# Block 0's first loads, the V blocks, the reciprocals and the last divisions of an adaLN transformer block put at other places in the program order

## The chip, the core and the metric

The kernel runs on one core of a Trainium2 chip. A core has five engines, each with its own instruction queue, worked off in order: TensorE (PE in the profile; its weight loads, PEld, overlap its matmuls), VectorE (DVE), ScalarE (ACT), GpSimd (POOL) and SyncE (SP), which here only issues DMAs. The metric is the device time of one execution in microseconds; lower is better. A measurement is a median of several runs.

## The reference, cut to what matters

`S = 2048` rows of width `D = 512`; attention with `H = 32` heads of 16; a feed-forward part of width 1792.

```python
mod = (_silu(c) @ w_mod).reshape(c.shape[0], 6, 1, -1)
sa, ca, ga, sb, cb, gb = (mod[:, i] for i in range(6))
h = _layernorm(x) * (1 + ca) + sa
qkv = (h @ wqkv)...                                # q, k, v of 32 heads of 16
p = _softmax(einsum("bhqd,bhkd->bhqk", q, k) * 16 ** -0.5)
x = x + ga * (einsum("bhqk,bhkd->bhqd", p, v)... @ wo)
h = _layernorm(x) * (1 + cb) + sb
x = x + gb * (gelu_tanh(h @ w1 + b1) @ w2 + b2)
```

## The kernel before

**Units and steps.** Queries are cut into 4 blocks of 512 rows (`NB`), heads into 8 groups of four. A pair of both is a *unit*: 32 units (`NU`), block by block. A unit goes over the 2048 keys in 16 *steps* of 128 keys (`NKC`), so the main loop has 512 steps (`half_step(hs)`, hs 0 to 511). A step has

- 4 score matmuls `e` (keys x queries) of its keys, each followed by an exponential on ScalarE (`p`); every exponential advances a counter, the *tick* (`advance`), so that a step has 4 ticks;
- 4 matmuls `mx` (queries x keys) of a later unit, 20 steps ahead, each followed by a reduction on VectorE to row maxima. When a unit has all 64 of them, `max_rows` combines them, POOL splits them in two parts, and they go to DRAM and back into two extra rows of the queries' tile `qst`, so that the score matmul itself subtracts them. The store is put 3 ticks, the load 6 ticks behind. For unit u this falls at the end of step 16u-5;
- the value matmuls `pv` of the step before, at the end of the step (`pv_step`), into one PSUM bank for the whole unit. At steps hs that are multiples of 16 this is the last step of a unit, and `attn_out` copies the bank to SBUF (`osb`) and sends it out;
- up to 6 *background* matmuls `bg` on half of the rows (`bg_mm`, `RUN`), from a generator of groups: in `block0` the projections of q, k and v, then per block of rows the output projection (`front`), the norm and the feed-forward part (`feed`). A group of 24 such matmuls takes four steps. A group starts only in an even step. A generator that yields `None` leaves the step without background.

**The order** is written by hand. `later(n, f)` runs `f` n ticks on; `sides` holds transposes of which one goes into a step. DMAs are all issued from SP's queue in program order. While the background fills the steps, each weight tile is fetched by `wload` into a ring of eight.

**Where the change bites.**

- `block0` ends when its last projection is stored (step 140 in the trace). `open_ffn` then takes over the memory of the staging tiles; four `wload` calls fetch the output weights `wo`; the generator waits `OPEN` ticks; `front(0)` has the rows x fetched into `x2` 9 ticks after that.
- V blocks: VectorE transposes the projected V in four blocks (`turn_blocks`, `turn_block`), two in each of two steps, from the single tile `vr`.
- `o_prep(b, k)` prepares the output projection of block b, a quarter k at a time: it loads denominators and sums, takes a reciprocal on VectorE (`inv`), sends it to DRAM (`store`), gets it back spread over the rows (`load`) and divides (`div`: a product, a cast and a difference on POOL; in the tail, `over`, on VectorE).
- `front(0)` after its four groups: the statistics and norm of the rows (`stat`, `factor`, `norm`) and four transposes (`trans`), each of 4 matmuls into a bank of the `mx` ring, a ScalarE pass and two POOL operations. The feed-forward groups follow when three are issued.
- A gelu is made in two halves (`ffn1`): a ScalarE pass and three POOL operations; 9 ticks later a tanh on ScalarE and four POOL operations (`second`).
- When the maxima of all units are done (step 492 on), the steps have no `mx` matmuls, four background matmuls and two exponentials in advance. From step 507 on no background group starts, and what is left of the feed-forward part of block 2 and all of block 3 run in a tail after the loop.

Of the kernel before, what the change touches and what calls it, by code (L numbers as in the profile page):

```python
# [10 lines left out]
AF = mybir.ActivationFunctionType  # L11
# [12 lines left out]
KC = D // P  # L24
NB = 4
# [34 lines left out]
Y202.a X1 x*2  # L60
"""
RUN = 6
OPEN = 12
WB = 8
FIRST = {"h32": 4, "pf": 1, "vr": 3}
STAGE = {"pf": 1, "vr": 1, "wraw": 2, "wf": 1}
# [6 lines left out]
def block_kernel(ctx: ExitStack, tc: tile.TileContext, x, wqkv, wo, w1, b1, w2, b2, c, w_mod, out):  # L73
# [276 lines left out]
    def turn_blocks(hs):  # L350
        if not blocked:
            return
        if until_hs[0] is None:
            until_hs[0] = hs + 1
        left = until_hs[0] - hs
        n = len(blocked)
        rowed_now = rowed[0] >= clock["t"] - 4
        for _ in range(n if left <= 0 else 0 if rowed_now and n <= 2 * left else -(-n // (left + 1))):
            turn_block()
# [66 lines left out]
        return reduce  # L426

    rows, rowed = {}, [0]

    def max_rows(u):  # L430
        rowed[0] = clock["t"]
# [272 lines left out]
    def attn_out(u, pv):  # L704
        qb, g = divmod(u, NG)
        o = kqpool.tile([P, TB], F32, tag="osb", name="osb", bufs=1)
        saw(ve.tensor_copy(o, pv))
        rowed[0] = clock["t"]
        late = u < NU - 1
        later(2 * late, lambda: sy.dma_start(ou_d[qb][g], o))  # L710
        if g % 2:
            later((4 if 0 < qb < NB - 1 and g == NG - 1 else 8) * late, lambda: ready.append((qb, g // 2)))
# [36 lines left out]
            return pools["f"].tile([P, D], F32, tag="t", name=name, bufs=8)  # L749
        return dvpool.tile([P, D], F32, tag="t", name=name, bufs=4)  # L750

    free_pc, busy, over = [0], [0], [False]

    def o_prep(b, k):

        dn = small.tile([P, 32], F32, tag="dn", name="dn")
        base = ou_d[b]
        sy.dma_start(dn, base[2 * k : 2 * k + 2].rearrange("g (j r) (a f) -> (g j) r a f", r=32, f=32)[:, DH])
        ob, rb = tmp("ob"), tmp("rb")
        for g in range(2):  # L760
            sy.dma_start(ob[g * 64 : (g + 1) * 64], base[2 * k + g].rearrange("(j r) t -> j r t", r=32)[:, :DH])
        eng = ve if over[0] else gp
        r = rden_d[b][k * 8 : (k + 1) * 8]
        busy[0] += 1

        def inv():
            ve.reciprocal(dn, dn)
            later(0 if over[0] else 2, store)

        def store():  # L770
            sy.dma_start(r.rearrange("h (a f) -> (h a) f", f=32), dn)
            later(1 if over[0] else 5, load)
            if over[0]:
                wload()

        def load():
            sy.dma_start(rb, bass.AP(tensor=r.tensor, offset=r.offset, ap=[[TB, 8], [0, DH], [1, TB]]))
            later(9 if over[0] else 3 if fast else 7, div)
            if k == KC - 1:
                later(2, lambda: close_by.__setitem__(b, True))  # L780
            if over[0]:
                for _ in range(6):
                    wload()
                load_x2(last, x2)

        def div():
            eng.tensor_tensor(ob, ob, rb, op=ALU.mult)
            eng.tensor_copy(pc(b, k, 0), ob)
            eng.tensor_tensor(pc(b, k, 1), ob, pc(b, k, 0).bitcast(F32), op=ALU.subtract)
            done[b] += 1  # L790
            busy[0] -= 1

        fast = 0 < b < NB - 1 and k == KC - 1
        later(11 if over[0] else 28 if b == 0 and k < KC - 1 else 9 if fast else 14, inv)

    def try_prep():
        if not ready or not pcs:
# [15 lines left out]
    for b in range(NB):  # L813
# [3 lines left out]
            at = top  # L817
        if b < NB - 1:
            stream += [(b + 1, "o", k) for k in range(KC)]
    wt, used, ringed, extra = {}, set(), [], []  # L820

    def wload():

        n = len(wt)
        if n == len(stream) or "f" not in pools:
            return
        key = stream[n]
        if extra:
            t = extra.pop()
        elif len(ringed) < WB or ringed[-WB] in used:  # L830
            t = pools["f"].tile([P, 2, D], FR, tag="w", name=f"w{key[1]}", bufs=WB)
            ringed.append(key)
        else:
            return
        sy.dma_start(t.bitcast(F32), {"o": wo_d, 1: w1_d, 2: w2_d}[key[1]][key[2]])
        wt[key] = t
# [19 lines left out]
    def front(b, x2):  # L856


        later(9, lambda: load_x2(b, x2))
        yield from until(lambda: close_by[b])  # L860
        yield from loaded(b, *[("o", k) for k in range(KC)])
        mv = small.tile([P, 4, 2], F32, tag="mv", name="mv")
        rs = {}
        xn = {}

        def norm(t):
            xn[t] = tmp("xn")
            (gp if b or t < 3 else ve).tensor_scalar(
                xn[t], x2[t], mv[:, t, 0:1], rs[t], op0=ALU.subtract, op1=ALU.mult)
            later(40 if b else 72, lambda: gp.tensor_tensor(x2[t], x2[t], b2_b, op=ALU.add))  # L870
            if len(xn) == 4:
                later(5, lambda: sides.extend([lambda fc=fc: trans(fc, "mx") for fc in range(KC)]))

        def stat(t):
            if b == 0 and t == 3:
                ln_stat(mv, t, x2[t])
                later(1, lambda: factor(t))
                return
            st = small.tile([P, 2, 6], F32, tag="bsh", name="bsh")

            def part(i):
                ve.bn_stats(st[:, i], x2[t][:, i * HD : (i + 1) * HD])

            def whole():
                ve.bn_aggr(mv[:, t], st)
                factor(t)

            def calm(f):
                later(3, f) if rowed[0] > clock["t"] - 4 else f()

            n = 4 if t < 3 else 3
            calm(lambda: [part(0), later(n, lambda: calm(lambda: [part(1), later(n, lambda: calm(whole))]))])

        def factor(t):
            rs[t] = small.tile([P, 1], F32, tag=f"rt{t}", name=f"rt{t}")
            ve.tensor_scalar(rs[t], mv[:, t, 1:2], EPS, None, op0=ALU.add)
            gp.tensor_tensor(rs[t], rs[t], mhalf[:, 0:1], op=ALU.pow)
            later(3 if t < 3 else 2, lambda: norm(t))

        for t in range(4):  # L900

            def evac(ps, t=t):
                y = tmp("y")
                ac.activation(y, ps, AF.Copy)

                def add():
                    gp.tensor_tensor(x2[t], y, x2[t], op=ALU.add)
                    later(8 if t < 3 else 4 if b else 3, lambda: stat(t))

                later(2, add)  # L910

            yield o_terms(b, t, range(KC)), "bg", evac
        drop(b, *[("o", k) for k in range(KC)])

        def trans(fc, bk):
            ps = take(bk)
            for t in range(4):
                te.transpose(ps[:, t * P : (t + 1) * P], xn[t][:, fc * P : (fc + 1) * P], ident)  # L918
            h = tmp("h32")
            ac.activation(h, ps, AF.Identity, scale=modc[:, 1, fc, 0:1], bias=modc[:, 1, fc, 1:2])  # L920
            gp.tensor_copy(pc(b, fc, 0), h)
            gp.tensor_tensor(pc(b, fc, 1), h, pc(b, fc, 0).bitcast(F32), op=ALU.subtract)
            turned[fc] = clock["t"]

        turned = {}
        yield "ln"
        yield from until(lambda: len(turned) >= KC - 1)

    def feed(b, x2):
# [7 lines left out]
        def ffn1(i):  # L937
            def evac(ps):
# [14 lines left out]
                def second():  # L953
# [5 lines left out]
                    gp.tensor_tensor(g[:, 1], h, g[:, 0].bitcast(F32), op=ALU.subtract)  # L959
                    gt[i] = g, clock["t"]  # L960

                later(9, second)

            wi = wt[b, 1, i].rearrange("p a (k n) -> p a k n", n=P)
# [40 lines left out]
    def block0():  # L1005

        plan = [(1, 1, [3]), (2, 1, [0, 1, 2, 3])]
        plan += [(w, k, range(1 if w == 0 else NB)) for k in (2, 3) for w in (0, 1, 2)]
        plan += [(0, k, range(1, NB)) for k in range(KC)]

        def fetch(n):
            if n < len(plan):
                w, k, _ = plan[n]
                load_w(w, k)
                soon(12, lambda: split_w(w, k, wslots[n % 4]))

        for key in [k for k in wt_of if k not in ((1, 1), (2, 1))]:
            wt_of.pop(key)
        for n, (w, k, bs) in enumerate(plan):
            if not pcs and not any(0 in p[2] for p in plan[n:]):  # L1020
                open_pc()
            yield from until(lambda: (w, k) in wt_of)
            fetch(n + 2)
            for b in bs:
                yield proj_v(k, b) if w == 2 else proj_qk(w, k, b, n == len(plan) - 1 and b == NB - 1)
            wt_of.pop((w, k))
        yield from until(lambda: not preps and not owed[0] and not blocked and not vrows and not busy[0])
        open_ffn()
        for k in range(KC):
            wload()  # L1030
        yield from wait(OPEN)

    pools["old"] = [dvcm, scm, wcm, hcm]

# [28 lines left out]
    def saw(ins):  # L1063

        if act["g"] and not act["g"]["seen"]:
            act["g"]["seen"] = ins.ins
# [285 lines left out]
```

## Time and profile before

| | us |
|---|---|
| timed runs | 1698.67, 1684.69, 1686.91; median 1686.91 |
| the profiled execution | 1683.93 |
| its span, first to last instruction | 1682.1, mean granted TensorE clock 0.993 |
| main loop, first to last value matmul | 106.3 to 1563.6 |
| tail, from the last value matmul | 1563.6 to 1682.1 |

In rows of the groups of instructions, "busy, mean ns of one" stands behind the count, then the idle time of the engine before them and what ended it. In rows of the time line the first number is the start in us from the span's start, the second the duration; brackets give the engine's idle time before it and its releaser. In rows of the chain a DMA's time runs from its issue to its landing. In rows of windows stand, after the stretch and its length, the busy times of PE, PEld, DVE, ACT and POOL with the count of instructions, the granted TensorE clock as a share, the DMA engines' busy share and the GB/s that they moved. In what follows, step n is the stretch that ends where the value matmuls of `half_step(n)` start; it holds the score matmuls of that step.

### The profile page before, as it was taken

What the parts mean: (1) busy time and instruction counts of PE and PEld (TensorE: products, weight loads), DVE (VectorE), ACT (ScalarE), POOL (GpSimd) and SP (SyncE); (2) the same over time, 40 slices, a digit from 0 to 9 for tenths busy, and PEclk for the clock granted to TensorE, in tenths of its full rate; (3) what the DMA queues carried; (4) which work ended last, traced back from release to release, by engine and by line L of the source; (5) the groups of instructions that cost most, each with busy time, mean ns of one, the idle gap of its engine ahead of it and who ended that gap; (6) DMA issues with size and microseconds to landing.
All of it is one profiled execution on the core that took longest, in us unless ns stands there. A gap on an engine that the chain in (4) does not pass through costs nothing.

```text
span 1682.1 us, 32274 instructions
## 1 busy us (share of the span) xinstructions
PE 1656.0 (98%) x12079; PEld 905.8 (54%) x12079; DVE 1424.9 (85%) x2770; ACT 1211.3 (72%) x2320; POOL 716.7 (43%) x719
## 2 busy tenths in 40 slices
PE   7999999999998999999999999999999999999999
PEld 6655555555544455555555555555555555553677
DVE  7999999999898999999999899999999899990332
ACT  4367777777776788778777888778777887788131
POOL 7443544534221376216523476126434475056210
PEclk8999999999999999999999999999999999999999
DMA  8766666665546443335462554254452643252544
GB/s 289 212 196 181 222 214 207 224 175 191 152 146 200 119 113 102 78 97 142 115 170 59 152 156 106 68 141 138 106 152 56 185 128 84 64 166 72 185 152 159
DMA packets 142808, 246.97 MB, mean 147 GB/s; under 512 B 25390, under 2 KB 53052, under 8 KB 142652
## 3 DMA queue, kind: packets, MB, share of 16 engines
q1 hardware_dynamic: 140896, 243.80, 49.8%
q8 instruction: 96, 1.57, 0.4%
q10 hardware_dynamic: 1756, 1.11, 0.3%
q14 instruction: 60, 0.49, 0.1%
HBM read 184.56 MB, written 60.29 MB: 146 GB/s over the span
## 4 chain that ended last, share of the span: by engine, by line
PE 93%; DMA 3%; DVE 2%; POOL 1%; ACT 0%; SPq 0%; issue 0%; POOLq 0%; ACTq 0%; DVEq 0%
PE bg L279 40%; PE pv L720 29%; PE e L685 16%; PE mx L415 4%; PE pr L279 2%; DMA wraw<-in_A_wqkv_dram 1%; DVE mxp L420 1%; PE o L279 1%; DMA qk<-parts 0%; DVE hTlo L510 0%; PE mx L918 0%; DMA m<-m 0%; DMA wt<-wos 0%; POOL wqkv L210 0%; DMA qst<-m 0%
## 5 line engine op out<-in xcount | busy, mean ns | idle before, releaser
L420 DVE TENSOR_REDUCE mxp<-mx 128x1 f32<-128x512 f32 x2038 | 1288.1, 682 | 116.7 <-PE mx L415 102.2
L692 ACT ACTIVATE p<-e 128x512 f32<-128x512 f32 x2048 | 1072.4, 608 | 307.9 <-PE mx L415 265.6
L415 PE MATMUL mx<-kh,qst 48*128 48x512 f32 x2038 | 842.2, 424 | 0.7 <-DVE mxp L420 0.5
L685 PE MATMUL e<-qst,kh 50*128 50x512 f32 x2048 | 777.3, 423 | 10.6 <-DMA qst<-m 5.3
L685 PEld LDWEIGHTS e<-qst,kh 50*128 50x128 f32 x2048 | 342.4, 185 | 440.6 <-ACT p L692 327.2
L720 PE MATMUL pv<-p,vg 128*17 128x512 f32 x4096 | 541.1, 599 | 0.1
L415 PEld LDWEIGHTS mx<-kh,qst 48*128 48x128 f32 x2038 | 369.8, 185 | 18.8 <-DVE mxp L420 9.4
L279 PE MATMUL bg<-w,g 64*128 64x512 f32 (+1 forms) x1080 | 269.7, 389 | 0.0
L279 PEld LDWEIGHTS bg<-w,g 64*128 64x128 f32 (+1 forms) x1080 | 200.4, 186 | 30.8 <-POOL g L958 0.9
L279 PE MATMUL bg<-pchi,w 64*128 64x512 f32 x672 | 182.9, 391 | 0.0
L720 PEld LDWEIGHTS pv<-p,vg 128*17 128x17 f32 x4096 | 68.2, 95 | 170.6 <-issue 168.8
L279 PE MATMUL bg<-hThi,wqkv 64*128 64x512 f32 x560 | 153.4, 393 | 0.0
L279 PEld LDWEIGHTS bg<-pchi,w 64*128 64x128 f32 x672 | 123.9, 185 | 23.0 <-DVE tick L1135 5.1
L279 PEld LDWEIGHTS bg<-hThi,wqkv 64*128 64x128 f32 x560 | 103.9, 186 | 12.4
L956 POOL TENSOR_SCALAR s<-s 128x512 f32<-128x512 f32 x42 | 62.9, 1497 | 82.5 <-ACT s L954 81.7
L279 PE MATMUL bg<-pclo,w 64*128 64x512 f32 x336 | 91.9, 392 | 0.0
L975 POOL TENSOR_TENSOR x<-y,x 128x512 f32<-128x512 f32 x28 | 36.0, 1286 | 125.5 <-ACT y L974 125.5
L279 PE MATMUL bg<-hTlo,wqkv 64*128 64x512 f32 x280 | 76.2, 391 | 0.0
L949 POOL TENSOR_TENSOR s<-h 128x512 f32<-128x512 f32 x42 | 43.8, 1042 | 74.9 <-ACT h L948 74.9
L279 PEld LDWEIGHTS bg<-pclo,w 64*128 64x128 f32 x336 | 61.7, 185 | 14.5 <-DVE tick L1135 3.4
L279 PE MATMUL bg<-wo,pchi 64*128 64x512 f32 x192 | 60.4, 395 | 0.0
L437 POOL CAST m<-mt 128x32 fp32r<-128x32 f32 x32 | 6.8, 212 | 123.1 <-DVE mt L435 123.1
(162 smaller groups left out, 1359.3 us busy)
## 6 DMA issues: line engine op xcount, KB each, us to landing
kh<-qk SPq DMA_DIRECT2D x256, 192.0 KB
w<-w2s SPq DMA_DIRECT2D x56, 512.0 KB
w<-w1s SPq DMA_DIRECT2D x54, 512.0 KB
qk<-parts SPq DMA_DIRECT2D x32, 512.0 KB
vg<-v SPq DMA_DIRECT2D x48, 272.0 KB
qst<-qk SPq DMA_DIRECT2D x64, 192.0 KB
qk<-parts SPq DMA_DIRECT2D x32, 256.0 KB
ou<-osb SPq DMA_DIRECT2D x32, 256.0 KB
```

The lines of the kernel that those rows point to most:

```text
L279: return te.matmul(ps, term[0][r], rhs, start=i == 0, stop=i == n - 1)
L415: te.matmul(ps, qst[u][r0 : r0 + KR, p, qc * P : (qc + 1) * P], kh(u, kr // 2)[r0 : r0 + KR, p, (kr % 2) * TB : (kr % 2 + 1) * TB], start= ...
L420: ins = ve.tensor_reduce(mxp[u][:, hc, kr : kr + 1], ps, axis=AX.X, op=ALU.max, negate=True)
L437: gp.tensor_copy(m2[:, 0], mt)
L685: ins = te.matmul(ps, kh(u, kc // 8)[r0 : r0 + KX, p, (kc % 8) * P : (kc % 8 + 1) * P], qst[u][r0 : r0 + KX, p], start=True, stop=True)
L692: op = ac.activation(t, ps, AF.Exp, scale=SCALE)
L720: te.matmul(pvb[32 * j : 32 * j + VW], vg[u % 2][:, n : n + VW], pt.pop(4 * s + j), start=kc == 0, stop=kc == NKC - 1)
L949: gp.tensor_tensor(s, h, h, op=ALU.mult)
L956: gp.tensor_scalar(s, s, 1.0, None, op0=ALU.add)
L975: later(4, lambda: gp.tensor_tensor(x2[t], y, x2[t], op=ALU.add))
```

## The change

- `block0` now waits `WAIT` = 6 ticks after `open_ffn` before it has the weights fetched (`wready` keeps the step's own `wload` calls back until then), fetches x of block 0 in the same place, and waits the other 8 of `OPEN` = 14 ticks.
- In the step at a unit's end `turn_blocks` turns no block.
- `calm`, which was local to the statistics, is shared: it puts an operation off by 2 ticks (it was 3) while VectorE has just been given a unit's combined maxima or copy, and now also in a unit's last step before `pv_step`. The reciprocals go through it.
- `attn_out` copies on ScalarE where no background group is under way.
- In `front(0)` the transposes are no longer all `sides`: two are given to the generator as steps of their own, in the background's bank, and the other two go as `sides` into the same two steps.
- The divisions of the last block wait (`behind`) for a tick that is 1 to 3 behind a gelu's first half, or more than 20 behind.

```diff
-OPEN = 12
+OPEN = 14
+WAIT = 6
...
         if until_hs[0] is None:
             until_hs[0] = hs + 1
+        if hs % NKC == 0:
+            until_hs[0] += 1
+            return
...
+    def calm(f):
+        if rowed[0] > clock["t"] - 4 or cur["pv"] % NKC == NKC - 1:
+            later(2, lambda: calm(f))
+        else:
+            f()
...
     def attn_out(u, pv):
         qb, g = divmod(u, NG)
         o = kqpool.tile([P, TB], F32, tag="osb", name="osb", bufs=1)
-        saw(ve.tensor_copy(o, pv))
-        rowed[0] = clock["t"]
+        if act["g"]:
+            saw(ve.tensor_copy(o, pv))
+            rowed[0] = clock["t"]
+        else:
+            ac.activation(o, pv, AF.Copy)
...
         def load():
             sy.dma_start(rb, bass.AP(tensor=r.tensor, offset=r.offset, ap=[[TB, 8], [0, DH], [1, TB]]))
-            later(9 if over[0] else 3 if fast else 7, div)
+            later(9 if over[0] else 3 if fast else 7, behind if b == NB - 1 and not over[0] else div)
...
+        def behind():
+            n = clock["t"] - gelu[0]
+            if over[0] or 1 <= n <= 3 or n > 20:
+                div()
+            else:
+                later(1, behind)
...
-        later(11 if over[0] else 28 if b == 0 and k < KC - 1 else 9 if fast else 14, inv)
+        later(11 if over[0] else 28 if b == 0 and k < KC - 1 else 9 if fast else 14, inv if over[0] else lambda: calm(inv))
...
     def wload():
         n = len(wt)
-        if n == len(stream) or "f" not in pools:
+        if n == len(stream) or "f" not in pools or not wready:
             return
...
     def front(b, x2):
-        later(9, lambda: load_x2(b, x2))
+        if b:
+            later(9, lambda: load_x2(b, x2))
...
             if len(xn) == 4:
-                later(5, lambda: sides.extend([lambda fc=fc: trans(fc, "mx") for fc in range(KC)]))
+                later(5, lambda: sides.extend([lambda fc=fc: trans(fc, "mx") for fc in range(KC)]) if b else normed.append(True))
...
-            def calm(f):
-                later(3, f) if rowed[0] > clock["t"] - 4 else f()
...
         yield "ln"
+        if b == 0:
+            yield from until(lambda: normed)
+            for fc in range(0, KC, 2):
+                sides.append(lambda fc=fc: trans(fc + 1, "mx"))
+                yield lambda fc=fc: trans(fc, "bg")
+            yield from until(lambda: len(turned) >= KC - 1)
+            return
         yield from until(lambda: len(turned) >= KC - 1)
...
+                gelu[0] = clock["t"]
                 later(9, second)
...
         open_ffn()
+        yield from wait(WAIT)
+        wready.append(True)
         for k in range(KC):
             wload()
-        yield from wait(OPEN)
+        load_x2(0, pools["x2"][0])
+        yield from wait(OPEN - WAIT)
```

More of the change, by code (lines that the diff above doesn't have):

```diff
@@ L750, in tmp @@
         return dvpool.tile([P, D], F32, tag="t", name=name, bufs=4)
-    free_pc, busy, over = [0], [0], [False]
+    free_pc, busy, over, gelu = [0], [0], [False], [-99]
     def o_prep(b, k):
@@ L819, in block_kernel @@
             stream += [(b + 1, "o", k) for k in range(KC)]
-    wt, used, ringed, extra = {}, set(), [], []
+    wt, used, ringed, extra, wready = {}, set(), [], [], []
     def wload():
         n = len(wt)
-        if n == len(stream) or "f" not in pools:
+        if n == len(stream) or "f" not in pools or not wready:
             return
@@ L863, in front @@
         rs = {}
-        xn = {}
+        xn, normed = {}, []
         def norm(t):
```

## The prediction

> **What bounds the kernel now.** I read the page's busy shares and chain first, then the times at which the value matmuls `pv` start, which mark the 512 steps, then every step that is longer than its neighbours.
>
> ```profile
> PE 1656.0 (98%) x12079; PEld 905.8 (54%) x12079; DVE 1424.9 (85%) x2770; ACT 1211.3 (72%) x2320; POOL 716.7 (43%) x719
> ...
> PE 93%; DMA 3%; DVE 2%; POOL 1%; ACT 0%; SPq 0%; issue 0%; POOLq 0%; ACTq 0%; DVEq 0%
> ```
>
> TensorE is the bound, and the change takes no matmul away. So only the steps in which TensorE waits can give time back. The next rows (length, then busy time of each engine, granted clock, DMA share and GB/s; one row for one step, except the fifth) hold those steps and what they should be compared with.
>
> ```profile
> 539.92:542.75 2.83, 2.83 (x26) 1.49 (x30) 2.76 (x7) 2.56 (x6) 1.30 (x2) 1.00 0.01 2
> 502.31:504.91 2.60, 2.38 (x18) 0.81 (x17) 2.55 (x5) 2.07 (x6) 0.55 (x3) 1.00 0.60 228
> 510.11:519.42 9.31, 4.47 (x24) 2.51 (x22) 3.51 (x6) 3.08 (x6) 0.00 (x0) 0.69 0.86 288
> 519.42:522.87 3.45, 3.45 (x24) 1.62 (x23) 2.52 (x5) 1.69 (x4) 0.00 (x0) 0.84 1.03 243
> 508.30:514.10 5.80, 2.64 (x20) 0.81 (x16) 3.13 (x6) 2.26 (x5) 0.00 (x0) 0.97 0.99 385
> 148.74:152.08 3.34, 3.31 (x25) 1.60 (x23) 3.34 (x9) 2.57 (x6) 0.00 (x0) 1.00 0.08 28
> 239.90:243.24 3.34, 3.31 (x25) 1.62 (x23) 3.34 (x9) 2.59 (x6) 2.29 (x3) 1.00 0.70 225
> 331.12:334.46 3.34, 3.31 (x25) 1.60 (x23) 3.34 (x9) 2.57 (x6) 0.59 (x1) 1.00 0.33 100
> 194.50:197.46 2.96, 2.96 (x25) 1.62 (x23) 2.96 (x7) 2.20 (x5) 2.54 (x3) 1.00 0.29 81
> 840.12:843.26 3.14, 3.14 (x24) 1.62 (x22) 3.14 (x8) 2.38 (x6) 0.00 (x0) 1.00 0.17 57
> 1206.56:1209.72 3.16, 3.16 (x24) 1.62 (x22) 3.16 (x8) 2.41 (x6) 0.00 (x0) 1.00 0.19 60
> 565.16:568.06 2.90, 2.60 (x18) 0.94 (x16) 2.87 (x8) 2.37 (x6) 2.80 (x2) 1.00 0.01 3
> 568.06:572.22 4.16, 3.65 (x21) 1.60 (x21) 4.16 (x9) 2.83 (x6) 0.56 (x1) 1.00 0.62 175
> 572.22:575.40 3.18, 2.96 (x22) 1.27 (x21) 2.72 (x5) 2.44 (x5) 1.89 (x2) 1.00 0.86 219
> 1513.35:1519.47 6.12, 3.07 (x20) 1.35 (x18) 1.71 (x6) 2.35 (x6) 5.53 (x8) 1.00 0.01 2
> 1519.47:1522.32 2.85, 2.85 (x17) 1.17 (x16) 0.16 (x1) 2.85 (x8) 2.62 (x4) 0.71 0.10 22
> 1522.32:1525.26 2.94, 2.94 (x16) 0.82 (x14) 0.16 (x1) 1.62 (x5) 1.17 (x1) 0.70 0.58 203
> 1529.48:1531.61 2.13, 2.13 (x18) 0.82 (x17) 0.85 (x2) 2.13 (x6) 1.66 (x2) 1.00 0.08 31
> ```
>
> An ordinary step with background matmuls takes 2.83 us, one without them 2.60. Two places stand out: step 144, the first of unit 9 (9.31 us), and step 492, the first after all maxima are done (6.12 us).
>
> **Step 144: output weights and x.** The queue of that place, and the landings that the chain shows:
>
> ```profile
> 502.90 0.46 SPq L302 DMA_DIRECT2D qk<-parts  x1
> ...
> 506.37 1.75 SPq L835 DMA_DIRECT2D wo<-wos  x4
> ...
> 508.17 1.16 SPq L442 DMA_DIRECT2D m<-m  x2
> ...
> 510.11 1.05 PE L720 MATMUL pv<-p,vg 128*17 128x512 f32 x8
> ...
> 514.32 0.57 SPq L448 DMA_DIRECT2D qst<-m  x2
> ...
> 515.99 0.76 PE L685 MATMUL e<-qst,kh 50*128 50x512 f32 x1 [4.83 <-DMA qst<-m]
> ```
>
> ```profile
> 416.13 1.95 DMA m<-m
> 418.13 2.81 DMA qst<-m
> ...
> 502.90 3.40 DMA qk<-parts
> ...
> 508.76 5.50 DMA m<-m
> 514.32 1.54 DMA qst<-m
> ```
>
> The four weight loads (512 KB each) go out at 506.37, as soon as the last projection has landed (502.90 + 3.40), and they stand in front of the store of unit 9's row maxima. That store takes 5.50 us instead of the 1.95 of unit 7; the maxima then reach the queries too late, and TensorE waits 4.83 us. The wait also costs clock: the granted share is 0.69 in this step and 0.84 in the next.
>
> In the new order the block's end (step 140) waits 6 ticks; a tick is one exponential, four to a step. Loads of weights and x then come in step 142, behind the maxima's store (step 140) and load (step 141). Background restarts 6+8 ticks after the end, at step 144 at the earliest. Before, 12 ticks gave step 143, which is odd, and a group begins only in an even step: so OPEN 14 costs no step. Steps 144 and 145 should take 2.83 + 2.96 (the row at 194.50 is the step after a unit's end) instead of 9.31 + 3.45: 6.97 us gained.
>
> What is late next: the weights. The maxima's store is free of the weights but not of the projection, so it lands at 506.3 to 507; the loads of the maxima go out then, take 1.54 to 2.81 us and land at 508 to 510, ahead of 511.1, when unit 9's first score matmul is due (510.11 plus 1.05 for the value matmuls of step 143). The weight loads follow on the queue, from about 507.2. At 385 GB/s (fifth row) 512 KB take 1.36 us. With 1.5 us around them (3.40 us less 2.0 us for the projection's 768 KB), the first quarter lands at about 510.1 and the second at 511.4; they are wanted at about 511.5 and 512.2. No wait is the lower end; if the loads go out 2 us later, the wait is 2 us. I take 0.4: **gain 6.6, between 3.5 and 7.0** (3.5: a wait of 2 us, and 1.5 of clock, below). The Trainium skill gives a price for a transfer (DMA: Bandwidth & Descriptors, Anatomy of one DMA): about 2.0 us plus bytes over 436 GB/s. As an estimate from it the two quarters land at 510.4 and 511.6, so there would be no wait, and the sum below would be 0.4 us lower.
>
> x (4 loads, 1 MB) and the weights (2 MB) now also stand in front of K of unit 10. At 385 GB/s 3.1 MB take 8.2 us, so K lands near 518; its maxima want it in step 148, at 511.1 + 4 x 2.83 = 522.4. Hidden, with 4 us to spare.
>
> **V blocks and reciprocals.** The three steps of 3.34 us hold two block transposes ahead of the copy of the finished unit, the two of 3.14 and 3.16 a reciprocal; VectorE is busy all through each. A unit's end without either takes 2.96. The copy itself, and a small item for the next part:
>
> ```profile
> L707 DVE COPY osb<-pv 128x512 f32<-128x512 f32 x32 | 21.7, 677 | 15.2 <-PE pv L720 15.2
> ...
> L885 DVE BATCH_NORM_AGGREGATE mv<-bsh 128x2 f32<-128x12 f32 x11 | 2.2, 200 | 0.0
> ```
>
> Moved one step on, they meet a VectorE that has 2.83 - 2.76 = 0.07 us free, but three banks of maxima between it and TensorE. Gain 3 x 0.38 = **1.1** and 0.18 + 0.20 = **0.4**. If they only lengthen the next step, nothing is gained; a second lengthening would cost as much (bounds -1.5 to 1.5). I take the gain, because the copy frees the only `pv` bank and a transpose frees none. The V store goes out one step later; its rows are wanted several steps on. A reciprocal is two steps later, with its store, load and division; the projection needs the division four steps after that.
>
> **Block 0's gap, steps 160 to 165.** It has no background. The copy of unit 9 goes from VectorE (0.68) to ScalarE, where 2.37 of 2.90 us are used. But the last statistics of row block 2 now fall in step 160, a unit's end, and are put off by four ticks. They then complete the norm one tick after step 163 has begun, so the four transposes, two to a step, come in steps 164 and 165 and background restarts at step 166, as before. By rows: steps 161 and 162 were 2.90 + 4.16, VectorE busy throughout; without the copy (0.68) but with the put-off aggregate (0.20) they take 6.6, or 5.9 if one maximum (0.68) more is left in its bank for later. Step 163 takes 2.60. One transpose group costs 3.18 - 2.60 = 0.58, so two give 3.76 a step, twice. Sum 16.0 to 16.7 against 2.90 + 4.16 + 3 x 3.18 = 16.6. Two transpose groups in one step show in no row, so the bounds are wider than that: **0, between -1 and +1**.
>
> **Step 492: the divisions.** POOL in program order, then who waits:
>
> ```profile
> 1507.83 0.70 ACT L948 ACTIVATE h<-bg,b_h 128x512 f32<-128x512 f32 x1
> ...
> 1511.45 1.30 POOL L787 TENSOR_TENSOR ob<-ob,rb 128x512 f32<-128x512 f32 x1
> ...
> 1513.51 1.29 POOL L789 TENSOR_TENSOR kh<-ob,kh 128x512 fp32r<-128x512 f32 x1
> ...
> 1516.58 1.26 POOL L951 TENSOR_TENSOR s<-s,h 128x512 f32<-128x512 f32 x1
> 1517.79 0.21 POOL L437 CAST m<-mt 128x32 fp32r<-128x32 f32 x1
> 1517.88 0.63 ACT L954 ACTIVATE s<-s 128x512 f32<-128x512 f32 x1 [3.77 <-POOL s L951]
> ...
> 1519.05 0.50 PE L685 MATMUL e<-qst,kh 50*128 50x512 f32 x1 [3.05 <-ACT p L692]
> ```
>
> The gelu's first half (from 1507.83) lies on POOL behind a division (1511.45 to 1514.80); its tanh waits 3.77 us at the head of ScalarE's queue, the exponentials wait behind it, and TensorE waits 3.05. In the new order both open divisions go out one tick behind that first half. POOL is then free for the half at once, the tanh finds it done, and steps 492 to 494 fall from 6.12 + 2.85 + 2.94 = 11.91 to 3.6 + 2 x 2.13 = 7.9. (3.6: this step issues two exponentials in advance, six, and ScalarE needs 2.07 for four in the 2.60 row: 3.1, and most of the tanh's 0.63.) **Gain 4.0, between 3.05, the bare wait, and 4.55, without the tanh.** Late next: two divisions, 6.6 us, from 1511.5, hold the maxima of unit 31 until 1518.1; that is what they had (1517.79), but their users now come some 4 us earlier, near 1523, with the load done at about 1523 (store 1.95, load 2.81). It just fits. The last division goes to the step before the last gelu, where ScalarE's queue is 2 us deep: nothing.
>
> **Sum.** 6.6 + 1.1 + 0.4 + 0 + 4.0 = 12.1 us off the profiled execution's 1683.93 gives 1671.8. The three timed runs begin 0.8 above that execution and their median is 3.0 above it; I add 1 and say **1673**.
>
> **Rivals.** *Weights late.* The wait only changes its name, from the maxima to the weights, at step 144: 2 us, with a lower clock behind it that costs 1.5 more (2.85 + 2.94 against 2 x 2.13, after a wait of 3.05). Gain there 3.5: 1676. For it: 2 MB wait for the maxima's landing. Against: the landings above. The Trainium skill (TensorE: Matmul & The Clock Gate, Part 1) lets the clock fall only after an idle window of some 3.4 us, so by it a 2 us wait would cost itself alone, and this rival would end at 1674.4. The trace differs: 3.05 us of waiting was followed by 0.71 and 0.70.
>
> *Maxima of unit 31 late.* Two divisions in a row instead of one: if their store takes 5.50 instead of 1.95, unit 31 waits 3.5 us, and most of step 492's gain is gone: 1676.3.
>
> *It doesn't do what it says.* The maxima are late from the projection, not from the weights, and the tanh late from POOL's whole load (5.53 of 6.12 us). Then 1.5 is left: 1683. Against: the store's issue at 508.17 stands directly behind the weights'.
>
> *Slower than before.* K of unit 10, behind 3.1 MB, misses step 148. Each us beyond 522.4 is lost; from a landing at 536.3 on it outweighs everything (1686.9 - 1673 = 13.9). At 70 GB/s 3.1 MB take 44 us and land at 553: 1673 + 30.6 = 1704. Against: that is less than a fifth of the 385 GB/s that this place shows.
>
> **How the numbers follow.** As forecast 0.60 (own range 1668 to 1677), weights late 0.15, unit 31 late 0.13, not as said 0.07, slower 0.05. All terms at their lower ends (3.5 - 1.5 - 1 + 3.05) leave 4 us, at their upper ends (7.0 + 1.5 + 1 + 4.55) 14: 1670 in the profiled execution's terms, less the 2.2 that lie between the two lower timed runs, 1667.5. The range 1667.5 to 1684 takes in the third rival and leaves out the slow one and the tails. About 1% is what a measurement of this kernel can tell from no change; 1% below 1686.91 is 1670.0, reached if all terms come in near their upper ends: a quarter of the forecast, 0.15. Above 1703.8 only the last rival could come: 0.04. The rest is within 1%.
>
> **What would show it.** Step 144 near 2.83 with `qst<-m` issued ahead of `wo<-wos`; a wait of `bg` on `wo` there speaks for the first rival. Steps 17, 49, 81, 257 and 385, behind units' ends, at 2.96. Steps 164 and 165 at 3.76, background from step 166; from 168 my tick count is wrong. Step 492 near 3.6 and no wait of the tanh on POOL; a wait on `qst<-m` at step 495 or 496 speaks for the second rival.

## The result and the profile after

| | before | after |
|---|---|---|
| timed runs, median us | 1686.57 (1684.69 to 1698.67, 4 runs) | 1670.51 (1669.34 to 1672.51, 4 runs) |
| ratio | | 0.9891, interval 0.9844 to 0.9938 |
| same program beside the last experiments | 1686.31 (6 runs) | 1672.81 (4 runs), ratio 0.9912, interval 0.9895 to 0.993 |
| profiled execution | 1683.93 | 1669.34 |
| its span | 1682.1 | 1667.6 |
| start to first `pv`, main loop, tail | 106.3, 1454.4, 121.4 | 104.7, 1441.7, 121.1 |

The kernel is about 1% faster. The main loop is 12.7 us shorter; here it is taken from the first start of a value matmul to the start of the last unbroken run of them (1560.71 before), and the tail from there. Here are the changed kernel's steps that answer to those shown of before, by the same view of windows (length, busy time of PE, PEld, DVE, ACT and POOL, granted clock, DMA share, GB/s): steps 17, 144, 145, 161 to 165, 257, 276, 385 and 492 to 495.

```profile
147.19:150.13 2.94, 2.94 (x26) 1.63 (x24) 2.94 (x6) 2.17 (x5) 0.00 (x0) 1.00 0.09 31
506.83:510.12 3.29, 3.19 (x24) 1.36 (x22) 3.04 (x6) 2.65 (x7) 0.00 (x0) 1.00 1.01 400
510.12:513.03 2.91, 2.91 (x24) 1.59 (x22) 2.79 (x6) 1.89 (x4) 0.00 (x0) 1.00 1.03 397
555.29:558.01 2.72, 2.39 (x19) 0.82 (x17) 2.65 (x9) 2.56 (x7) 0.16 (x1) 1.00 0.05 18
558.01:561.64 3.63, 2.98 (x18) 1.09 (x17) 3.63 (x6) 2.82 (x7) 3.00 (x3) 1.00 0.80 211
561.64:564.24 2.60, 2.38 (x17) 0.84 (x16) 2.60 (x6) 1.42 (x4) 0.00 (x0) 1.00 0.88 211
564.24:568.04 3.80, 3.80 (x27) 1.83 (x25) 3.80 (x7) 3.27 (x8) 0.00 (x0) 1.00 1.06 268
568.04:571.53 3.49, 3.49 (x25) 1.64 (x24) 2.24 (x5) 3.10 (x6) 3.29 (x4) 1.00 0.85 179
829.92:832.86 2.94, 2.94 (x25) 1.61 (x23) 2.94 (x7) 2.17 (x5) 0.00 (x0) 1.00 0.09 33
883.97:886.95 2.98, 2.98 (x24) 1.59 (x22) 2.95 (x9) 2.22 (x6) 0.88 (x2) 1.00 0.73 166
1196.55:1199.48 2.93, 2.93 (x25) 1.61 (x23) 2.93 (x6) 2.15 (x5) 0.00 (x0) 1.00 0.15 55
1503.34:1505.99 2.65, 2.65 (x21) 1.36 (x19) 1.71 (x6) 2.34 (x6) 2.57 (x3) 1.00 0.00 0
1505.99:1508.11 2.12, 2.12 (x17) 0.82 (x16) 0.16 (x1) 2.12 (x6) 1.98 (x3) 1.00 0.03 8
1508.11:1510.22 2.11, 2.11 (x16) 0.80 (x14) 0.16 (x1) 2.11 (x6) 1.95 (x4) 1.00 0.05 8
1510.22:1513.34 3.12, 2.39 (x17) 0.73 (x16) 0.16 (x1) 3.12 (x7) 2.89 (x4) 1.00 0.24 42
```

The 9.31 us of step 144 and the 6.12 of step 492 are gone, and so is the halved clock behind both. Step 495 is new: 3.12 us where it was 2.11. The queue at step 144, from the time line:

```profile
500.12 1.56 SPq L452 DMA_DIRECT2D m<-m  x2
...
503.60 0.57 SPq L458 DMA_DIRECT2D qst<-m  x2
...
504.36 1.76 SPq L855 DMA_DIRECT2D wo<-wos  x4
...
506.16 2.67 SPq L874 DMA_DIRECT2D x<-in_A_x_dram  x4
...
508.87 1.00 SPq L391 DMA_DIRECT2D kh<-qk  x2
509.23 0.18 PEld L280 LDWEIGHTS bg<-wo,pchi 64*128 64x128 f32 x1 [0.53 <-DMA wo<-wos]
```

The maxima's store goes out at 500.12, ahead of the weights, and their load at 503.60. What is late now is the second quarter of the weights: its weight load waits 0.53 us, and the step takes 3.29 us where an ordinary one takes 2.83. POOL at step 492, with those who wait for it:

```profile
1500.42 1.28 POOL L976 TENSOR_TENSOR s<-s,h 128x512 f32<-128x512 f32 x1
...
1501.66 1.29 POOL L807 TENSOR_TENSOR ob<-ob,rb 128x512 f32<-128x512 f32 x1
...
1503.96 0.65 ACT L979 ACTIVATE s<-s 128x512 f32<-128x512 f32 x1
...
1504.95 1.29 POOL L807 TENSOR_TENSOR ob<-ob,rb 128x512 f32<-128x512 f32 x1
...
1508.24 0.20 POOL L447 CAST m<-mt 128x32 fp32r<-128x32 f32 x1
...
1511.13 0.57 SPq L458 DMA_DIRECT2D qst<-m  x2
...
1512.67 0.73 PE L695 MATMUL e<-qst,kh 50*128 50x512 f32 x2 [0.73 <-DMA qst<-m]
```

The gelu's first half ends at 1501.70 and its tanh (L979) waits for nothing. Both divisions follow, and the split of unit 31's maxima (L447) comes behind them at 1508.24. Its load is issued at 1511.13, and TensorE waits 0.73 us for it; the step grows by 1.0.

### The profile page after: what moved, and what is told of

It reads as the page before. It is cut to its first block, busy times and chain, and to the rows that moved or that the text cites. A ratio compares the mean times of both kernels' runs of the same rounds, so it can differ in the third digit from the quotient of the medians.

```text
span 1667.6 us, 32273 instructions
## 1 busy us (share of the span) xinstructions
PE 1647.8 (99%) x12079; PEld 901.6 (54%) x12079; DVE 1421.1 (85%) x2768; ACT 1212.2 (73%) x2322; POOL 716.9 (43%) x719
## 4 chain that ended last, share of the span: by engine, by line
PE 94%; DMA 2%; DVE 2%; ACT 1%; POOL 0%; issue 0%; SPq 0%; POOLq 0%; DVEq 0%
PE bg L280 39%; PE pv L733 30%; PE e L695 17%; PE mx L419 5%; PE pr L280 2%; DVE mxp L424 1%; PE o L280 1%; DMA wm<-in_w_mod_dram 1%; DVE bst L238 0%; PE mx L936 0%; DMA wt<-wos 0%; DMA rden<-dn 0%; DMA m<-m 0%; DMA wo<-wos 0%; PE pr L233 0%
## 5 line engine op out<-in xcount | busy, mean ns | idle before, releaser
L447 POOL CAST m<-mt 128x32 fp32r<-128x32 f32 x32 | 6.8, 212 | 123.1 <-DVE mt L445 123.1
```

The lines of the kernel that those rows point to most:

```text
L447: gp.tensor_copy(m2[:, 0], mt)
```

## The experiments

In the diffs below, `...` stands for lines left out: declarations, and what the whole change has as well.

**One part at a time, on the kernel before.** The first has the loads moved, and nothing else:

```diff
-OPEN = 12
+OPEN = 14
+WAIT = 6
...
-        later(9, lambda: load_x2(b, x2))
+        if b:
+            later(9, lambda: load_x2(b, x2))
...
         open_ffn()
+        yield from wait(WAIT)
+        wready.append(True)
         for k in range(KC):
             wload()
-        yield from wait(OPEN)
+        load_x2(0, pools["x2"][0])
+        yield from wait(OPEN - WAIT)
```

> The kernel before with the first part alone: output weights and x of block 0 fetched behind the row maxima of unit 9. Theory (the weights in front of the maxima's store made TensorE wait): step 144 falls from 9.31 to about 3.3 us and step 145 from 3.45 to about 2.9, 6.5 us in all, and steps 162 to 165 and 492 stay as before (4.16, 3.18, 6.12). Rival (the projection's own store made the maxima late): step 144 stays above 8 us. Whole time: 6.5 us less by the theory, no change by the rival.

Measured: ratio 0.9963, interval 0.995 to 0.9976 (1679.63 against 1686.51). Its steps 144, 145 and 492 to 494:

```profile
509.33:512.60 3.27, 3.24 (x25) 1.36 (x23) 3.06 (x6) 2.66 (x6) 0.00 (x0) 1.00 0.99 386
512.60:515.51 2.91, 2.91 (x24) 1.59 (x23) 2.78 (x6) 1.89 (x4) 0.00 (x0) 1.00 1.03 390
1506.25:1513.46 7.21, 3.36 (x20) 1.46 (x18) 1.71 (x6) 2.64 (x6) 6.55 (x9) 0.84 0.01 2
1513.46:1517.30 3.84, 3.84 (x17) 1.30 (x16) 0.16 (x1) 2.81 (x7) 3.48 (x4) 0.50 0.37 110
1517.30:1519.73 2.43, 2.43 (x17) 0.82 (x15) 0.16 (x1) 1.48 (x4) 0.00 (x0) 0.85 0.36 124
```

The projection's store was in place as before, and the wait is gone: it was the weights. The last three rows show something not looked for. Nothing was changed there, and yet these steps take 13.48 us instead of the 11.91 of the first profile, at a lower clock.

The second has the divisions alone:

```diff
...
-            later(9 if over[0] else 3 if fast else 7, div)
+            later(9 if over[0] else 3 if fast else 7, behind if b == NB - 1 and not over[0] else div)
...
```

> The kernel before with the last part alone: the divisions of the last block behind a gelu's first half. Theory (a division in front of the half makes the tanh late, and the exponentials behind it): step 492 falls from 6.12 to about 2.6 us, 493 and 494 from 2.85 and 2.94 to about 2.1, and step 495 rises from 2.11 to about 3.1 because the maxima of unit 31 now lie behind both divisions: 4.0 us less. Rival (POOL is simply full there): step 492 stays above 5 us, as the same POOL work is done. Steps 144 and 145 stay at 9.31 and 3.45.

Measured: ratio 0.9966, interval 0.9952 to 0.998 (1680.69 us). Steps 492 to 495 are 2.65, 2.11, 2.11 and 3.23 us, so the same POOL work in another order costs nothing at step 492 and about a microsecond at 495. The theory holds. By these steps against the first profile 3.9 us are gained (14.02 to 10.10); the whole is 5.8 us less (1680.69 against 1686.51), which fits the other executions of the old order: they take longer there, as the first experiment's does.

The third has V blocks and reciprocals alone; the statistics keep their own `calm`, and `quiet` is the shared one:

```diff
+        if hs % NKC == 0:
+            until_hs[0] += 1
+            return
...
-        later(11 if over[0] else 28 if b == 0 and k < KC - 1 else 9 if fast else 14, inv)
+        later(11 if over[0] else 28 if b == 0 and k < KC - 1 else 9 if fast else 14, inv if over[0] else lambda: quiet(inv))
```

> The kernel before with V blocks and reciprocals kept out of the unit-end steps, nothing else. Theory (what counts is what stands before the copy of the finished unit on VectorE): steps 17, 49 and 81 fall from 3.34 to 2.95, steps 257 and 385 from 3.15 to 2.94, and no step behind them grows: 1.6 us less. Rival (VectorE's work is only moved): the steps behind grow by as much, 0 us. Step 112 was 3.44 before and 2.85 after the whole change; if it is 2.85 here, the moved reciprocals did that, if 3.44, another part or chance.

Measured: steps 17, 49, 81, 257 and 385 at 2.95, 2.95, 2.94, 2.96 and 2.91; no step behind them is longer (step 18 is 2.83). The whole, 1687.0 us, doesn't show it, since steps 492 to 494 happened to take 13.92 us in this execution. Step 112 is 2.83 here, but so it is in the first two experiments, which move no reciprocal.

The fourth has the copy on ScalarE and the transposes two to a step:

```diff
+        if act["g"]:
             saw(ve.tensor_copy(o, pv))
             rowed[0] = clock["t"]
+        else:
+            ac.activation(o, pv, AF.Copy)
...
+                sides.append(lambda fc=fc: trans(fc + 1, "mx"))
+                yield lambda fc=fc: trans(fc, "bg")
```

> The kernel before with only the copy on ScalarE where no background runs and the transposes of block 0 two to a step. Theory (the gap is bound by VectorE while the copy is there, and by TensorE and ScalarE in the steps with transposes): steps 161 to 165 sum to 16.2 us instead of 16.6, the two steps with transposes at 3.6 to 3.8 and background again from step 166. Rival (pairing the transposes is what saves): one background step more, from step 164 or 165. Steps 144 and 492 stay as before.

Measured, steps 161 to 165: 2.73, 2.91, 4.00, 3.50 and 2.60, together 15.74 us against 16.61 before and 16.24 after the whole change. Background starts again at step 166 in all three. So the gain here is 0.87, and something else in the change takes 0.5 back. The gain lies in steps 161 and 162 (7.06 to 5.64), and 163 to 165 lose (9.55 to 10.10); how much of either is the copy's and how much the pairing's was not run apart. 1686.29 us in all, with steps 492 to 494 at 13.97.

**Which differences are chance.** The kernel before, unchanged, profiled a second time:

> The kernel before, profiled a second time, to see which differences between the two profiled executions are chance. Theory: the start (first value matmul at 106.29 us before, 104.75 after the change) and step 112 (3.44 and 2.85) hang on DMAs from memory and vary from one execution to the next, by 1 us or more at the start; steps 17, 144, 162 and 492 repeat within 0.1 us (3.34, 9.31, 4.16, 6.12). Rival: start and step 112 repeat too; then the change moved them.

Measured: first value matmul at 105.56, step 112 2.83, steps 17 and 162 as before, 144 at 9.49. But steps 163 and 492 don't repeat:

```profile
571.23:575.62 4.39, 4.39 (x23) 1.68 (x22) 2.83 (x5) 2.56 (x5) 1.88 (x2) 0.61 0.95 251
567.93:571.34 3.41, 2.89 (x20) 1.58 (x20) 3.41 (x7) 2.17 (x4) 0.00 (x0) 1.00 0.75 203
1513.33:1520.13 6.80, 3.06 (x21) 1.35 (x19) 1.69 (x6) 2.34 (x6) 6.14 (x9) 1.00 0.01 2
1520.13:1523.82 3.69, 3.69 (x17) 1.28 (x16) 0.16 (x1) 3.01 (x8) 3.46 (x4) 0.54 0.30 65
1523.82:1525.93 2.11, 2.11 (x16) 0.80 (x14) 0.16 (x1) 1.57 (x5) 0.33 (x1) 1.00 0.58 195
```

Step 163 takes 4.39 us at a clock of 0.61, where the first profile has 3.18 at 1.00; the clock fell after a stretch of 3.41 us in which TensorE was busy for 2.89 (second row). Steps 492 to 494 take 12.60. The changed kernel a second time, beside the last experiments:

> The changed kernel again, beside the mended ones on the same chip. Theory: start, step 112 and step 294 (104.7, 2.85 and 3.18 us in its first profile) are chance and come out elsewhere (105 to 107, 2.83, 2.82), while steps 144, 161 to 165, 276, 404 and 495 repeat within 0.1 us (3.29, 16.24 together, 2.98, 2.98, 3.11).

Measured: first value matmul at 106.63, step 294 at 2.83, steps 276, 404 and 161 to 165 as in the first profile, 144 at 3.29, 495 at 3.18. The main loop agrees with the first profile's within 0.1 us; its span is 1672.2, of which 1.9 lie in the start and 2.8 in the tail, where the clock is halved once for 3.41 us.

**The small losses.** The changed kernel, with the old rule for the statistics:

```diff
+            def calm(f):
+                later(3, f) if rowed[0] > clock["t"] - 4 else f()
+
             n = 4 if t < 3 else 3
```

> The changed kernel, but the statistics of the norm keep their own rule of being put off (3 ticks, no look at the unit's last step). Theory (the new losses at steps 276 and 404, 2.98 instead of 2.84, and at 294, 3.18 instead of 2.82, come from statistics put at other ticks): these three go back to 2.84, 2.84 and 2.82, 0.64 us less in the main loop; block 0's transposes come a step earlier, in 163 and 164, and background still restarts at step 166. Rival (they are chance or belong to the reciprocals): the three steps stay at 2.98, 2.98 and 3.18.

Measured: steps 276, 294 and 404 at 2.83 each; steps 161 to 165 sum to 15.7. For 276 and 404 and the gap the theory holds: with the shared rule VectorE has nine operations in step 276 and is busy for 2.95 of 2.98 us (row above), with the old one eight. Step 294 was chance, as the repetition shows: it is 2.83 there with the shared rule.

One division behind a gelu:

```diff
...
-            if over[0] or 1 <= n <= 3 or n > 20:
+            if over[0] or 1 <= n <= 3 and not taken[0] == gelu[0] or n > 20:
+                taken[0] = gelu[0]
                 div()
```

> The changed kernel, but only one division of the last block goes behind a gelu's first half; the second waits until the tick count allows it. Theory (step 495 is 3.11 us instead of 2.11 because the maxima of unit 31 stand behind two divisions on POOL): the split of the maxima starts 3.3 us earlier, step 495 falls to about 2.1, steps 492 to 494 stay at 2.64, 2.13 and 2.11, 1.0 us less in all. Rival (step 495's wait is the store and load of the maxima, with or without POOL): step 495 stays above 2.8. If the second division meets the next gelu, a wait of about 1 us near step 497 takes the gain back.

Measured: step 495 at 2.11, 492 to 494 as after, step 498 at 2.30 instead of 2.12. The wait was POOL's order; 0.18 of the 1.0 us comes back at 498.

**The price of late weights, and of late x.**

```diff
-WAIT = 6
+WAIT = 10
```

> The changed kernel with WAIT 10 instead of 6: the weights go out one step later, step 144 still being the first that needs them. Theory (each us of later weights is a us of waiting, as the cover is used up): step 144 grows from 3.29 by one step's 2.6 us to 5.9 us. On the clock: the Trainium skill (TensorE: Matmul & The Clock Gate, Part 1) has it fall after an idle window of 3.4 us, so a wait of 3.1 us should leave steps 144 and 145 at a granted clock of 1.00; by the trace of before, where 3.05 us of waiting was followed by 0.71 and 0.70, the clock falls and step 145 or 146 is 0.5 to 1.5 us longer. Rival to the first: the weights come so fast that step 144 stays below 4 us.

Measured: 1675.07 us; step 144 and step 145, and the 3.41 us before the clock fell:

```profile
507.65:514.50 6.85, 4.38 (x24) 1.86 (x22) 3.50 (x6) 3.06 (x6) 0.00 (x0) 0.81 1.00 358
514.50:517.80 3.30, 3.30 (x25) 1.62 (x24) 2.53 (x5) 1.72 (x4) 0.00 (x0) 0.88 1.11 304
508.48:511.89 3.41, 0.94 (x8) 0.51 (x6) 1.29 (x3) 0.74 (x2) 0.00 (x0) 1.00 0.98 364
```

A matmul waits 2.46 us for the first quarter, and one more weight load 0.64 for the second, while the matmuls before it still run: of step 144's 6.85 us TensorE's matmuls are idle for 2.47, of the changed kernel's 3.29 for 0.10. Then it runs at half clock. The two steps cost 3.56 + 0.38 = 3.9 us more, of which 2.4 are the longer wait and some 1.5, by subtraction, the clock. Step 144 was expected at 5.9, for the wait alone. Late weights cost more than their lateness. The Trainium skill's page that the expectation names (TensorE: Matmul & The Clock Gate, Part 1) would have kept the clock up; the trace has it fall, to 0.81 over step 144 and 0.88 over step 145.

```diff
-        if b:
-            later(9, lambda: load_x2(b, x2))
+        later(9, lambda: load_x2(b, x2))
...
-        load_x2(0, pools["x2"][0])
```

> The changed kernel, but x of block 0 is fetched 9 ticks behind the start of the block, as before, so that only the weights stand there in the queue. Step 144 waits 0.53 us for the weights in the changed kernel. Theory (transfers of one queue share the DMA engines, so x and K slow the second quarter of the weights): the wait goes, step 144 at 2.85 instead of 3.29. Rival (the queue works in order and the wait is the issue at 504.4 plus the weights' own time): step 144 stays within 0.1 us of 3.29.

Measured: the theory fell, step 144 stays at 3.29. But step 150 takes 6.94 us and the whole 1676.81. The chain of waits there, from the time line:

```profile
519.65 1.09 SPq L874 DMA_DIRECT2D x<-in_A_x_dram  x2
...
529.15 1.26 POOL L924 TENSOR_TENSOR x<-y,x 128x512 f32<-128x512 f32 x1 [28.56 <-DMA w<-w1s]
...
530.45 0.43 DVE L902 BATCH_NORM_STATS2 bsh<-x 128x6 f32<-128x256 f32 x1 [3.86 <-POOL x L924]
...
531.52 0.79 PE L419 MATMUL mx<-kh,qst 48*128 48x512 f32 x1 [3.37 <-DVE mxp L424]
```

x stands behind K, V and the next weights now and lands when step 150's statistics already stand in VectorE's queue; VectorE waits 3.86 us for the sum on POOL, the maxima's banks fill, and TensorE waits 3.37. (The releaser given for POOL here is the weights' load; the last x load was issued at 520.4 and lies in the same queue. In the trace of the last version below, which also has x late, the same sum waits for x itself:)

```profile
530.57 1.26 POOL L928 TENSOR_TENSOR x<-y,x 128x512 f32<-128x512 f32 x1 [28.07 <-DMA x<-in_A_x_dram]
```

Before the change x was just as late: its loads went out from 517.66 (here from 516.50) and the sum ran at 529.37 (here at 529.15). The 6.5 us lost at step 144 covered it. So x's early place is no by-work of this change. In this trace steps 150 to 152 lose 6.7 us without it, all that the loads gained.

**A version with both mends** (old rule for the statistics, one division), and the same with x late:

> The changed kernel with both mends: the statistics keep their own rule, and one division of the last block goes behind a gelu's first half. Theory (the mends are independent): steps 161 to 165 at 15.7 instead of 16.24, 276 and 404 at 2.83, 495 at 2.11, so the main loop is 1.8 us shorter than the changed kernel's, and the whole near 1668 where the changed kernel takes 1670. Rival (the steps gained are given back in the tail, which waits for the last division): the main loop is shorter and the whole is not.

> The kernel with both mends and x of block 0 late. If x slows the weights, step 144 at 2.85 and the main loop 2.2 us shorter than the changed kernel's; if not, as the kernel with both mends, 1.8 us shorter.

Measured, for the first, steps 161 to 165:

```profile
556.46:559.21 2.75, 2.41 (x18) 0.84 (x16) 2.72 (x7) 2.59 (x7) 2.75 (x2) 1.00 0.06 20
559.21:562.11 2.90, 2.90 (x18) 1.17 (x16) 2.90 (x6) 2.33 (x5) 0.59 (x2) 1.00 0.77 193
562.11:566.12 4.01, 4.00 (x26) 1.83 (x25) 4.01 (x8) 3.11 (x7) 0.01 (x1) 1.00 0.98 220
566.12:569.62 3.50, 3.50 (x26) 1.65 (x25) 2.25 (x5) 3.06 (x6) 3.34 (x4) 1.00 1.05 246
569.62:572.22 2.60, 2.38 (x19) 0.81 (x18) 1.59 (x3) 2.50 (x6) 2.52 (x4) 1.00 0.93 212
```

They sum to 15.8 against 16.24; 276 and 404 are at 2.84, 495 at 2.11. The main loop is 1440.1 us against 1441.7: 1.6 less, where 1.8 were expected. In time it is 1670.1 us, ratio to before 0.9905 (0.9889 to 0.9921), beside 1672.81 and 0.9912 for the change itself on the same chip: the intervals overlap, so the times don't show what the steps show. The tail's variation (121 to 124 us) is larger. With x late the wait at step 150 comes back (6.14 us), and steps 150 to 152 lose some 4.9 us. That profiled execution took 1676.60; the other three took 1670.34 to 1672.98, and the median of all four is 1672.88, 2.8 above the same version with x early. So a late x costs 5 to 7 us in the two traces; by their times it costs the executions without a trace less.

## Why the prediction was right, point by point

The forecast was 12.1 us less: 1671.8 in the profiled execution and 1673 as a median; measured were 1669.34, and 1670.51 and 1672.81 as medians. In the steps:

| place | forecast | first profiles |
|---|---|---|
| 144, 145 (weights and x) | 6.6 | 9.31 + 3.45 - 3.29 - 2.91 = 6.56 |
| 17, 49, 81 (V blocks) | 1.1 | 1.17 |
| 257, 385 (reciprocals) | 0.4 | 0.44 |
| 161 to 165 (gap) | 0 | 0.37 |
| 492 to 495 (divisions) | 4.0 | 5.03 at 492 to 494, less 1.01 at 495 |
| 276, 404 | none | -0.28 |
| start, step 112, step 294 (chance) | none | 1.55 + 0.59 - 0.36 |

The rows sum to 14.1 of the 14.6 us between the two profiled executions, and 1.8 of them are chance; step 498 and the tail make up the rest.

- *Step 144* came out by its own steps: maxima ahead of the weights, OPEN 14 free of cost, the second quarter of the weights late. That the size fits is partly luck. The prediction's rows had this quarter land at 511.4 and wanted at 512.2, which is no wait; the 0.4 was a choice between that and 2 us. In the trace it landed at 509.19 (issued at 504.75, under way for 4.44), which is 512.47 when counted on the time line of before (step 143 ends 3.28 us earlier now): 1.1 us later than worked out. The estimate by the Trainium skill's price of a transfer (DMA: Bandwidth & Descriptors, Anatomy of one DMA) gave no wait either, and the trace has one; that section's price is for transfers issued from GpSimd, and these are issued from SyncE. K of unit 10 stayed hidden (step 148 at 2.84). What the prediction didn't see is that x had to move: it costed x only as a load in K's way, never as one that is late. That the change fetches it early kept the 6.6, for a reason that the prediction doesn't give.
- *V blocks and reciprocals* held: what stood ahead of the copy of `pv` was the cost, and the moved work was absorbed.
- *The gap* held in its schedule (transposes in 164 and 165, background from 166). The copy and pairing alone are worth 0.87 (15.74 against 16.61); the aggregate put off by the shared rule takes 0.5 back.
- *The divisions*: the sum held, but two of its sizes were off and cancelled. Step 492 takes 2.65 and not 3.6: six exponentials were charged to the step, but they run on into the next ones (ScalarE is busy for 2.34, 2.12 and 2.11 us of steps 492 to 494) and TensorE doesn't wait for them. And "it just fits" failed: unit 31's maxima came 0.73 us late behind two divisions, which is the second rival in small. Its mechanism is shown by the version with one division. (That rival's 1676.3 should be 1676.5 by its own numbers, 1673 + 3.5.)
- *The base*: the first profile of before had steps 492 to 494 cheaper than any other execution with the same order there: 11.91, against 12.60, 13.48, 13.92 and 13.97. So against these executions the divisions gain 1 to 2 us more than forecast. Steps 144 and 145 were cheap there too: 12.76, against 13.27, 13.41, 13.42 and 13.63 in the four other traces with the old order of the loads.

## What to carry to other kernels

In a queue that is worked off in order, a big load that is wanted late can stand in front of a tiny one that is wanted now; put the tiny one first, but then look for the next use of everything that was delayed by the old wait: x was covered by it, and cost 5 to 7 us at the next place in the traces with x late. On an engine with a strict order, the same work behind a half that others wait for costs nothing, and in front of it costs the wait and the clock; here two such pieces in a row already missed the next deadline by 0.73 us. When parts of a change are small, read them step by step from the trace: the time of a whole run varied here by 4.4 us (1669.63 to 1673.99), more than all parts but the two largest.

## What the hardware showed beyond that

A long wait costs TensorE more than itself, and not always the same; the short ones, 0.53 us at step 144 and 0.73 at step 495, left the granted clock at 1.00. The clock fell after a wait of 2.46 us (busy 0.94 of the 3.41 us before), and once after a stretch with 2.89 of 3.41 us busy, while the same step kept its clock in another execution. It came back after one or two such stretches (3.41 us or 6.83); the price of the same wait at step 492 was between 11.91 and 13.97 us for three steps. Which share of busy time decides wasn't measured. The tail too had such a stretch in three executions (the kernel before and the changed one, each a second time, and the third experiment), worth some 2.5 us; its cause stays open.
